# Attention and feed-forward on one core: the second feed-forward product as seven block products for each pair of batches

## Chip, core and metric

The kernel runs on one core of a Trainium2 chip. TensorE is PE in the profile, VectorE DVE, ScalarE ACT, GpSimd POOL, and SyncE, which issues all DMAs here, SP. The metric is the device time of one execution in microseconds (us).

## What is computed

Attention over 8 batches of 12 heads (448 rows of 64), and a feed-forward layer over the 3584 rows of 768 that come out of it. Everything is float32 (or float64 weights, which are decoded first). Cut to what matters here:

```python
q_n, k_n = rmsnorm(q, g_q), rmsnorm(k, g_k)
attn = softmax(q_n @ k_n.T / 8)          # 8 batches x 12 heads, 448 x 448
x = (attn @ v).reshape(3584, 768)
h = x @ w_in                             # 3584 x 2048
g = h * np.cos(h)
y = g @ w_out                            # 2048 x 768
```

## The kernel before

The program has two stages, each with its own plan. A plan (`Plan`) is a list of steps; `add` names a step's engine, its cost, when it is due, and which tiles it reads and writes. `order` plays the list through with one clock for each engine: of the steps that could start, an engine takes the one that is due first. Rings (`RING`, `RING2`) say how many buffers a kind of tile has. What comes out is a fixed order of instructions on each engine. The plan reckons the five engines as independent: a step of DVE costs the same whether POOL is at work or not. Costs are numbers written in the code (`add(DVE, 1.66, ...)`).

Products are made with float32 operands split in two float32r parts, hi and lo: ACT casts hi (`nc.scalar.copy`), POOL or DVE subtracts it from the operand for lo, and PE does three matmuls, hi by hi, hi by lo and lo by hi, into one PSUM bank.

First stage, to about 979 us: the attention, by pairs of heads, and h = x @ w_in of batches 0 to 6 fitted between (`ffn1`, lines 547 to 549, slices `fc` of 128 of the 2048 columns, 16 of them). h goes to DRAM (`h_out`, `h_store`, tile `h_d`). `weights2` brings w_out in 32 halves of a slice, decodes it (DVE, and one step of ACT), splits it (`v_split`: ACT line 261, POOL line 263) and stores both parts in DRAM (`wo_d`).

Second stage: PE begins with h of the last batch (`ffn1_block`, 16 slices of 18 matmuls of 448 columns). As each slice is through, its place in SBUF takes a slice of w_out (`v_place`, 768 KB, from `wo_d`). All 16 slices are then resident. The rows are taken in 7 groups of 512 (`CT`), whatever their batch. For each group and each two slices (a block of 128 x 1024):

- SP loads h (`gl_load`, line 569);
- `g_turns`: how many turns h is, rounded by adding a large number (DVE, line 576), made into the amount to take off (POOL, line 578);
- `g_reduce`: two instructions on DVE (lines 584 and 586) bring h to within half a turn;
- `g_cos`: absolute value and sine on ACT (lines 590, 591);
- `g_mul`: h times cosine on DVE (line 595);
- `g_split`: hi on ACT (line 604), lo on POOL (line 602);
- `ffn2` on PE (lines 618 to 620): for each slice, 6 output blocks x 3 matmuls of 512 columns, summed over 16 slices in 6 PSUM banks.

At the end of a group ACT and DVE take turns to copy the six banks (`y_out`, lines 632 and 634), and SP stores them.

Of the kernel before, what the change touches and what calls it, by code (L numbers as in the profile page):

```python
# [126 lines left out]
def tile_attention_moe(  # L127
# [115 lines left out]
    def v_fetch(fc, hf):
        cs = slice(hf * HM, hf * HM + HM)
        st = apool.tile([128, DM], I32, tag="wf", name=f"rawo{fc}_{hf}", bufs=RING["wf"])
        f = apool.tile([128, DM], F32, tag="wf", name=f"wo{fc}_{hf}", bufs=RING["wf"])
        half[(fc, hf)] = (st, f[:, :HM])
        if f64:
            nc.sync.dma_start(st, w_out[fc][:, cs].bitcast(I32))
        else:  # L250
            nc.sync.dma_start(f[:, :HM], w_out[fc][:, cs])

    def v_decode(fc, hf, step):
        st, f = half[(fc, hf)]
        if f64:
            decode(st, f, step)

    def v_split(fc, hf, lo):
        st, f = half[(fc, hf)]
        if not lo:  # L260
            nc.scalar.copy(st.bitcast(F32R)[:, :HM], f)
        else:
            nc.gpsimd.tensor_tensor(st.bitcast(F32R)[:, HM:], f, st.bitcast(F32)[:, :HM], ALU.subtract)
# [301 lines left out]
    gts = {}

    def gl_load(b, gi):
        hb = gpool.tile([128, NG, CT], F32, tag="hb", name=f"hb{b}_{gi}", bufs=4)
        nc.sync.dma_start(hb, h_d[gi * NG : gi * NG + NG, :, b * CT : b * CT + CT].rearrange("f p s -> p f s"))
        gts[(b, gi)] = {"h": hb}  # L570

    def g_turns(b, gi, step):
        d = gts[(b, gi)]
        if step == 0:
            n = d["n"] = gpool.tile([128, NG, CT], F32, tag="n", name=f"n{b}_{gi}", bufs=2)
            nc.vector.tensor_scalar(n, d["h"], 1.0 / (2.0 * math.pi), MAGIC, op0=ALU.mult, op1=ALU.add)  # L576
        else:
            nc.gpsimd.tensor_scalar(d["n"], d["n"], -MAGIC, -C1, op0=ALU.add, op1=ALU.mult)  # L578

    def g_reduce(b, gi, step):  # L580
        d = gts[(b, gi)]
        if step == 0:
# [1 line left out]
            nc.vector.tensor_tensor(r, d["h"], d["n"], ALU.add)  # L584
        else:
            nc.vector.scalar_tensor_tensor(d["r"], d.pop("n"), C2 / C1, d["r"], op0=ALU.mult, op1=ALU.add)  # L586

    def g_cos(b, gi):
        r = gts[(b, gi)]["r"]
        nc.scalar.activation(r, r, AF.Abs)  # L590
        nc.scalar.activation(r, r, AF.Sin, bias=halfpi, scale=-1.0)

    def g_mul(b, gi):
        d = gts[(b, gi)]
        nc.vector.tensor_tensor(d["r"], d["r"], d.pop("h"), ALU.mult)

    def g_split(b, gi, lo):
        d = gts[(b, gi)]
        t = gpool.tile([128, NG, CT], F32R, tag="glo" if lo else "ghi", name=f"g{lo}{b}_{gi}")
        d["lo" if lo else "hi"] = t  # L600
        if lo:
            nc.gpsimd.tensor_tensor(t, d.pop("r"), d["hi"].bitcast(F32), ALU.subtract)  # L602
        else:
            nc.scalar.copy(t, d["r"])  # L604

    ys = {}

    def ffn2(b, fc):
        d = gts[(b, fc // NG)]
        hi, lo = d["hi"][:, fc % NG, :], d["lo"][:, fc % NG, :]  # L610
        w = wts[("wo", fc)]
        for oc in range(NOC):
# [5 lines left out]
            nc.tensor.matmul(y, whi, hi, start=(fc == 0), stop=False)  # L618
# [1 line left out]
            nc.tensor.matmul(y, wlo, hi, start=False, stop=(fc == NFC - 1))  # L620
# [303 lines left out]
```

## Time and profile before

| | us |
|---|---|
| median of 3 runs (1504.03 to 1506.16) | 1504.94 |
| the profiled execution, its own time | 1502.19 |
| its span in the profile | 1500.1 |
| PE busy | 1453.1 |
| DVE busy | 1036.8 |
| ACT busy | 867.3 |
| POOL busy | 848.5 |

How to read it: a line of the page or of a group names the engine, the line of the kernel, the operation, and output <- input by the program's names; x56 is a count. Where three figures stand with strokes between, they are the shortest, the median and the longest of one instruction in ns. A window row gives its length and then, for each engine, the busy time in it and in brackets the number of instructions; the last three figures are the clock granted to PE, the share of time in which the DMA engines were busy, and what they moved in GB/s. A timeline row gives start and duration in us; in square brackets stands how long the engine was idle before it, and what ended that. Matmuls are pipelined: one of 512 columns lasts 0.39 us and the next starts 0.23 us after it. An instruction that waits inside, after it was issued, counts as busy.

### The profile page before, as it was taken

Reading aid. Unit: us, or ns where it says so; the run is one execution under the profiler, and the core shown is the slowest. Engines: PE = TensorE matmul, PEld = TensorE weight load, DVE = VectorE, ACT = ScalarE, POOL = GpSimd, SP = SyncE. Lnnn points to the kernel's source line nnn. Section 1 sums busy time; section 2 is a strip of 40 time slices with the busy share of each in tenths; the row PEclk is TensorE's granted clock in tenths of the full one; section 3 lists DMA queues with packets and bytes.
Section 4 is the critical chain, followed back from the end, with each engine's and each line's share of the span. In section 5 each row is a group of like instructions: output and inputs, shape, how many; then the busy total and the mean of one; then the engine's idle time right before and its main releaser. Section 6 shows DMA issues by size and latency. Waiting matters only on the chain.

```text
span 1500.1 us, 21753 instructions
## 1 busy us (share of the span) xinstructions
PE 1453.1 (97%) x7404; PEld 1164.9 (78%) x7404; DVE 1036.8 (69%) x1856; ACT 867.3 (58%) x1736; POOL 848.5 (57%) x678
## 2 busy tenths in 40 slices
PE   7898998999999999999999999999999999999998
PEld 3446786878788878877887888788888888888887
DVE  7878999778777777877777765452566665665660
ACT  5777777677767766766666675442343443434431
POOL 5779789766856756855655462042344444454441
PEclk8999999999999999999999999999999999999999
DMA  6576424556455555544454441177232323323221
GB/s 201 175 227 223 124 84 139 184 174 174 156 160 177 153 152 165 151 151 144 152 167 127 125 127 60 64 275 278 56 100 70 99 83 98 99 71 98 71 71 42
DMA packets 113919, 204.28 MB, mean 136 GB/s; under 512 B 19008, under 2 KB 73104, under 8 KB 113808
## 3 DMA queue, kind: packets, MB, share of 16 engines
q1 hardware_dynamic: 113808, 202.90, 43.3%
q8 instruction: 58, 0.95, 0.3%
q14 instruction: 53, 0.43, 0.1%
HBM read 149.55 MB, written 53.29 MB: 135 GB/s over the span
## 4 chain that ended last, share of the span: by engine, by line
PE 77%; DVE 6%; ACT 3%; issue 3%; POOL 2%; DMA 1%; ACTq 0%; POOLq 0%; DVEq 0%
PE y L618 10%; PE y L619 10%; PE y L620 10%; PE ph L547 9%; PE ph L548 8%; PE ph L549 8%; PE O L502 8%; PE PT L466 7%; PE S L421 6%; ACT hi L477 1%; DVE lo L485 1%; DVE S L428 1%; DVE xf L519 1%; DVE hi L487 1%; DVE wo L217 1%
## 5 line engine op out<-in xcount | busy, mean ns | idle before, releaser
L547 PE MATMUL ph<-xs,wi 128*128 128x448 f32 x768 | 298.7, 389 | 3.2 <-ACT he L559 3.2
L548 PE MATMUL ph<-xs,wi 128*128 128x448 f32 x768 | 282.1, 367 | 1.2 <-DVE xs L533 1.2
L549 PE MATMUL ph<-xs,wi 128*128 128x448 f32 x768 | 281.3, 366 | 0.0
L441 ACT ACTIVATE P<-S,sm 128x448 f32<-128x448 f32 x336 | 214.1, 641 | 100.1 <-DVE S L428 89.2
L618 PE MATMUL y<-g,wo 128*128 128x512 f32 x672 | 262.5, 391 | 0.0
L620 PE MATMUL y<-g,wo 128*128 128x512 f32 x672 | 261.5, 389 | 0.0
L619 PE MATMUL y<-g,wo 128*128 128x512 f32 x672 | 261.5, 389 | 0.0
L428 DVE TENSOR_SCALAR_CACHE_REDUCE S<-S,nr 128x448 f32<-128x448 f32 x336 | 219.4, 684 | 17.6 <-PE S L421 16.1
L602 POOL TENSOR_TENSOR g<-r,g 128x1024 fp32r<-128x1024 f32 x56 | 140.9, 2516 | 156.1 <-ACT g L604 156.0
L477 ACT CAST hi<-PT 128x448 fp32r<-128x448 f32 x336 | 164.7, 536 | 83.6 <-PE PT L466 45.5
L485 DVE TENSOR_TENSOR lo<-PT,hi 128x448 fp32r<-128x448 f32 x252 | 145.3, 617 | 77.6 <-ACT hi L477 76.7
L466 PEld LDWEIGHTS PT<-ident,P 128*128 128x128 f32 x1344 | 156.5, 141 | 33.7 <-issue 22.8
L466 PE MATMUL PT<-ident,P 128*128 128x128 f32 x1344 | 181.9, 276 | 0.1
L547 PEld LDWEIGHTS ph<-xs,wi 128*128 128x128 f32 x768 | 144.7, 188 | 34.5 <-issue 13.0
L590 ACT ACTIVATE r<-r 128x1024 f32<-128x1024 f32 x56 | 59.4, 1061 | 167.7 <-DVE r L586 167.5
L584 DVE TENSOR_TENSOR r<-hb,n 128x1024 f32<-128x1024 f32 x56 | 83.6, 1493 | 103.6 <-POOL g L602 102.3
L549 PEld LDWEIGHTS ph<-xs,wi 128*128 128x128 f32 x768 | 144.5, 188 | 12.4
L548 PEld LDWEIGHTS ph<-xs,wi 128*128 128x128 f32 x768 | 145.1, 189 | 11.4 <-DVE xs L533 2.0
L299 POOL TENSOR_TENSOR r<-r,nhalf 128x14 f32<-128x14 f32 (+1 forms) x50 | 127.4, 2550 | 40.5 <-DVE r L295 30.5
L618 PEld LDWEIGHTS y<-g,wo 128*128 128x128 f32 x672 | 126.1, 188 | 28.7 <-ACT ye L632 1.3
L578 POOL TENSOR_SCALAR n<-n 128x1024 f32<-128x1024 f32 x56 | 76.7, 1370 | 125.7 <-DVE n L576 124.6
L620 PEld LDWEIGHTS y<-g,wo 128*128 128x128 f32 x672 | 126.1, 188 | 26.3
(83 smaller groups left out, 2584.0 us busy)
## 6 DMA issues: line engine op xcount, KB each, us to landing
h_d<-he SPq DMA_DIRECT2D x128, 224.0 KB
hb<-h_d SPq DMA_DIRECT2D x56, 512.0 KB
sd<-sd SPq DMA_DIRECT2D x46, 448.0 KB
vd<-v SPq DMA_DIRECT2D x84, 160.0 KB
qd<-qT SPq DMA_DIRECT2D x48, 256.0 KB
raw<-w_in SPq DMA_DIRECT2D x16, 768.0 KB
...
```

What stands on the lines that cost most here:

```text
L428: nc.vector.tensor_scalar(d["S", t][:, :S], d["S", t][:, :S], d["nr"][:, t : t + 1], None, op0=ALU.mult, op1=ALU.min, accum_out=d["sm"][:, ...
L441: nc.scalar.activation(tl(u, f"P{t}", [128, S], F32, "P"), d.pop(("S", t))[:, :S], AF.Exp, bias=sm[:, 1, t : t + 1], scale=-1.0, accum_out ...
L466: nc.tensor.transpose(pt[:, t * 128 : t * 128 + 128], src, ident)
L477: nc.scalar.copy(hi, pt[:, hh * S : hh * S + S])
L485: nc.vector.tensor_tensor(lo, src, hi.bitcast(F32), ALU.subtract)
L547: nc.tensor.matmul(ph[:, :S], whi, x2[:, 0, :], start=(cc == 0), stop=False)
L548: nc.tensor.matmul(ph[:, :S], whi, x2[:, 1, :], start=False, stop=False)
L549: nc.tensor.matmul(ph[:, :S], wlo, x2[:, 0, :], start=False, stop=(cc == NCC - 1))
L602: nc.gpsimd.tensor_tensor(t, d.pop("r"), d["hi"].bitcast(F32), ALU.subtract)
L618: nc.tensor.matmul(y, whi, hi, start=(fc == 0), stop=False)
L619: nc.tensor.matmul(y, whi, lo, start=False, stop=False)
L620: nc.tensor.matmul(y, wlo, hi, start=False, stop=(fc == NFC - 1))
```

## The change

Batches are taken in pairs. For a pair, g is seen as a 2 x 2 matrix of blocks (which half of the 2048 columns of g; which batch), and w_out as 2 x 2 blocks (which half of its 2048 rows: X, Y; which half of its 768 columns: 1, 2). The four output blocks come from seven products of blocks instead of eight. In the code, a and b are the first half of g for the first and second batch of the pair, c and d the second half for the first and second. Products in order: a by X1; b - a by X2 + Y2; then b, now holding d - b, by X1 - X2; d, a (d less the former a), c, and a (less c) by the other three combinations and Y1, Y2. Each is 8 slices x 3 output blocks x 3 matmuls of 448 columns.

The parts of the change:

- `weights2`, first stage: for each of 8 slices, four quarter pieces are fetched and decoded as before, POOL makes four combinations (`v_mix`), and seven results are split and stored: 56 splits on ACT and on POOL, 32 mixes on POOL, 56 stores, where 32 splits and 32 stores stood.
- `v_place`: the weights of products 0 and 1 stay resident in 8 places. Those of products 2 to 6 are loaded anew for each pair into the other 8, two slices (768 KB) at a time: 16 loads at first, as before, and 72 more while the products run.
- `g_turns` is one instruction on ACT that writes an int32. DVE's line 576 and POOL's line 578 go.
- `g_reduce`, `g_cos`, `g_mul` work on blocks of 128 x 896, 64 in all. Their result stays in SBUF in float32 (tiles B, four homes of four blocks); rings: 3 buffers for h, 5 for hi, 4 for lo.
- `g_mix`: 16 blocks for each pair are combined, 12 on DVE and 4 on POOL.
- `g_split` is done for each slice of each product: 224 casts on ACT and 224 subtractions on POOL of 128 x 448.
- `e_copy` (36 on ACT), `e_add` (48 on DVE, reading PSUM) and `e_sum` (36 on DVE, both inputs in SBUF) put the outputs together.
- `h_d` is laid out by batch, and the scratch for dynamic DMA is set to 1024.

The change, cut:

```diff
-    h_d = dpool.tile([NFC, 128, B * S], F32, tag="h_d", name="h_d")
-    wo_d = dpool.tile([NFC, 128, 2, DM], F32, tag="wo_d", name="wo_d")
+    h_d = dpool.tile([B, NFC, 128, S], F32, tag="h_d", name="h_d")
+    NH = NFC // 2
+    NPR = 7
+    wo_d = dpool.tile([NH, NPR, 128, 2, HM], F32, tag="wo_d", name="wo_d")
...
+        "wx": 5, "wv": 2,
...
+    X1, X2, Y1, Y2, SS = range(5)
+    ORDER = (1, 5, 7, 3, 6, 2, 4)
...
+    def v_mix(k, to, a, c, op):
+        if to == SS and (k, SS) not in mix:
+            mix[(k, SS)] = apool.tile([128, HM], F32, tag="wx", name=f"wx{k}_{SS}", bufs=RING["wx"])
+        nc.gpsimd.tensor_tensor(mix[(k, to)], mix[(k, a)], mix[(k, c)], op)
...
+    def v_split(k, p, m, lo):
         if not lo:
-            nc.scalar.copy(st.bitcast(F32R)[:, :HM], f)
-        else:
-            nc.gpsimd.tensor_tensor(st.bitcast(F32R)[:, HM:], f, st.bitcast(F32)[:, :HM], ALU.subtract)
-
-    def v_store(fc, hf):
-        st, _ = half.pop((fc, hf))
-        cs = slice(hf * HM, hf * HM + HM)
-        nc.sync.dma_start(wo_d[fc][:, :, cs], st.bitcast(F32).rearrange("p (a n) -> p a n", a=2))
-
-    def v_place(fc):
-        w = wts[("wo", fc)] = wpool.tile([128, 2, DM], F32R, tag=f"w{fc}", name=f"wo{fc}")
-        nc.sync.dma_start(w.bitcast(F32), wo_d[fc])
+            t = vts[(k, p)] = apool.tile([128, 2, HM], F32R, tag="wv", name=f"wv{k}_{p}", bufs=RING["wv"])
+            nc.scalar.copy(t[:, 0, :], mix[(k, m)])
+        else:
+            t = vts[(k, p)]
+            nc.gpsimd.tensor_tensor(t[:, 1, :], mix[(k, m)], t.bitcast(F32)[:, 0, :], ALU.subtract)
...
+    def v_place(pr, pi, kk, slot):
+        w = wts[("wo", slot)] = wpool.tile([128, 2, 2, HM], F32R, tag=f"w{slot}", name=f"wo{pr}_{pi}_{kk}")
+        nc.sync.dma_start(w.bitcast(F32), wo_d[2 * kk : 2 * kk + 2, pi].rearrange("f p a n -> p f a n"))
...
+    def g_turns(pr, role, g):
+        n = blk[(pr, role, g, "n")] = gpool.tile([128, NG, S], I32, tag="n", name=f"n{pr}{role}{g}", bufs=RING2["n"])
+        nc.scalar.activation(n, gts[(pr, role, g)], AF.Copy, scale=1.0 / (2.0 * math.pi))
...
+            nc.vector.scalar_tensor_tensor(
+                t, blk[(pr, role, g, "n")], -C1, gts[(pr, role, g)], op0=ALU.mult, op1=ALU.add
...
+            nc.vector.scalar_tensor_tensor(t, blk.pop((pr, role, g, "n")), -C2, t, op0=ALU.mult, op1=ALU.add)
...
+    def g_mix(pr, to, a, c, g, eng):
+        t = blk[(pr, to, g)]
+        eng.tensor_tensor(t, blk[(pr, a, g)], blk[(pr, c, g)], ALU.subtract)
+
+    def g_split(pr, pi, role, k, lo):
+        t = gpool.tile([128, S], F32R, tag="glo" if lo else "ghi", name=f"g{lo}{pr}{pi}{k}", bufs=RING2["glo" if lo else "ghi"])
+        ops[(pr, pi, k, lo)] = t
+        src = blk[(pr, role, k // NG)][:, k % NG, :]
         if lo:
-            nc.gpsimd.tensor_tensor(t, d.pop("r"), d["hi"].bitcast(F32), ALU.subtract)
-        else:
-            nc.scalar.copy(t, d["r"])
-
-    ys = {}
-
-    def ffn2(b, fc):
-        d = gts[(b, fc // NG)]
-        hi, lo = d["hi"][:, fc % NG, :], d["lo"][:, fc % NG, :]
-        w = wts[("wo", fc)]
-        for oc in range(NOC):
-            if fc == 0:
-                ys[(b, oc)] = ps_y.tile([128, 512], F32, tag="y", name=f"y{b}_{oc}")
-            y = ys[(b, oc)]
+            nc.gpsimd.tensor_tensor(t, src, ops[(pr, pi, k, 0)].bitcast(F32), ALU.subtract)
+        else:
+            nc.scalar.copy(t, src)
...
+    def ffn2(pr, pi, k, slot):
+        hi, lo = ops.pop((pr, pi, k, 0)), ops.pop((pr, pi, k, 1))
+        w = wts[("wo", slot)][:, k % 2]
+        for oc in range(NO):
+            if k == 0:
+                ys[(pr, pi, oc)] = ps_y.tile([128, 512], F32, tag="y", name=f"y{pr}_{pi}_{oc}")
+            y = ys[(pr, pi, oc)][:, :S]
...
+            nc.tensor.matmul(y, whi, hi, start=(k == 0), stop=False)
             nc.tensor.matmul(y, whi, lo, start=False, stop=False)
-            nc.tensor.matmul(y, wlo, hi, start=False, stop=(fc == NFC - 1))
-
-    yes = {}
-
-    def y_out(b, oc, hf=None):
-        y = ys[(b, oc)]
-        if (b, oc) not in yes:
-            yes[(b, oc)] = gpool.tile([128, CT], F32, tag=f"ye{oc}", name=f"ye{b}_{oc}", bufs=1)
-        ye = yes[(b, oc)]
-        if hf is not None:
-            y, ye = (t[:, hf * CT // 2 : hf * CT // 2 + CT // 2] for t in (y, ye))
-        if (hf if hf is not None else oc) % 2 == 0:
-            nc.scalar.copy(ye, y)
-        else:
-            nc.vector.tensor_copy(ye, y)
-
-    def y_store(b, oc):
-        nc.sync.dma_start(out[oc * 128 : oc * 128 + 128, b * CT : (b + 1) * CT], yes.pop((b, oc)))
+            nc.tensor.matmul(y, wlo, hi, start=False, stop=(k == NH - 1))
...
+    def e_copy(pr, pi, oc, name):
+        nc.scalar.copy(e_tile(pr, name, oc), ys.pop((pr, pi, oc))[:, :S])
+
+    def e_add(pr, pi, oc, to, a, op):
+        y = ys.pop((pr, pi, oc))[:, :S]
+        if op == ALU.add:
+            nc.vector.tensor_tensor(e_tile(pr, to, oc), y, e_tile(pr, a, oc), op)
+        else:
+            nc.vector.tensor_tensor(e_tile(pr, to, oc), e_tile(pr, a, oc), y, op)
+
+    def e_sum(pr, oc, to, a, eng):
+        t = e_tile(pr, to, oc)
+        eng.tensor_tensor(t, t, e_tile(pr, a, oc), ALU.add)
...
+        todo = ((1, X1, None), (2, Y1, None), (4, Y2, None), (5, SS, (X2, Y2, ALU.add)), (7, X2, (X1, X2, ALU.subtract)),
+                (6, SS, (SS, X1, ALU.subtract)), (3, Y1, (Y1, SS, ALU.subtract)))
+        for n, (p, m, ab) in enumerate(todo):
+            e = d + n * span / 14.0
+            if ab:
+                add(POOL, 1.05, e, v_mix, k, m, *ab, r=[x[i] for i in ab[:2] if i != m], w=[x[m]])
+            t = ("wv", NPR * k + n)
+            add(ACT, 0.5, e + 3.0, v_split, k, p, m, False, r=[x[m]], w=[t])
+            add(POOL, 1.05, e + 5.0, v_split, k, p, m, True, r=[x[m]], w=[t])
+            add(SP, ISS, e + 9.0, v_store, k, p, r=[t], land=LAND)
...
+    NGR, NO = NH // NG, NOC // 2
+    ROLES = {"a": (0, 0), "b": (0, 1), "d": (1, 1), "c": (1, 0)}
+    RING2 = {"he": 2, "hb": 3, "n": 2, "ghi": 5, "glo": 4, "y": 8}
...
+    def slot(pr, pi, kk):
+        return 4 * pi + kk if pi < 2 else 8 + (20 * pr + 4 * (pi - 2) + kk) % 8
...
+    def block(pr, role, g, d):
+        i, j = ROLES[role]
+        n = next(count)
+        hb, t = ("hb", n), ("n", n)
+        B_ = ("B", home(pr, role), g)
+        r = [("hd", 2 * pr + j, NH * i + NG * g + f) for f in range(NG)]
+        add(SP, ISS, d - 30.0, gl_load, pr, role, g, r=r, w=[hb], land=LAND)
+        add(ACT, 0.95, d - 20.0, g_turns, pr, role, g, r=[hb], w=[t])
+        add(DVE, 1.15, d - 17.0, g_reduce, pr, role, g, 0, r=[hb, t], w=[B_])
+        add(DVE, 1.15, d - 16.0, g_reduce, pr, role, g, 1, r=[t], w=[B_])
+        add(ACT, 2.0, d - 14.0, g_cos, pr, role, g, w=[B_])
+        add(DVE, 1.2, d - 11.0, g_mul, pr, role, g, r=[hb], w=[B_])
...
+    def product(pr, pi, role):
+        d0 = T0 + PROD * (NPR * pr + pi)
+        for kk in range(NH // 2):
+            if pi >= 2 or pr == 0:
+                s = slot(pr, pi, kk)
+                add(SP, ISS, d0 + 2 * PART * kk - 24.0, v_place, pr, pi, kk, s, w=[("w", s)], land=8.0)
+        for k in range(NH):
+            d = d0 + PART * k
+            n = next(split_n)
+            B_, hi, lo = ("B", home(pr, role), k // NG), ("ghi", n), ("glo", n)
+            add(ACT, 0.53, d - 7.0, g_split, pr, pi, role, k, 0, r=[B_], w=[hi])
+            add(POOL, 1.25, d - 5.0, g_split, pr, pi, role, k, 1, r=[B_, hi], w=[lo])
+            s = slot(pr, pi, k // 2)
+            add(PE, PART, d, ffn2, pr, pi, k, s, r=[hi, lo, ("w", s)], w=[("y", Y(pr, pi, oc)) for oc in range(NO)])
+        return d0 + PROD
...
+    for pr in range(NPAIR):
+        D = [T0 + PROD * (NPR * pr + pi) for pi in range(NPR + 1)]
+        gs_ = range(NGR)
+        for role, pi in (("a", 0), ("b", 1), ("d", 2), ("c", 5)):
+            for g in gs_:
+                block(pr, role, g, D[pi] + BLOCK * g - (9.0 if role != "a" else 0.0))
+        copies(pr, 0, "e1", product(pr, 0, "a") + 2)
+        for g in gs_:
+            mix(pr, "a", "b", "a", g, DVE, D[1] + BLOCK * g - 10.0)
+        copies(pr, 1, "e5", product(pr, 1, "a") + 2)
+        for g in gs_:
+            mix(pr, "b", "d", "b", g, POOL, D[2] + BLOCK * g - 12.0)
+        copies(pr, 2, "e7", product(pr, 2, "b") + 2)
+        for g in gs_:
+            mix(pr, "a", "d", "a", g, DVE, D[4] + BLOCK * g - 14.0)
+        sums(pr, 3, "e3", "e5", ALU.add, product(pr, 3, "d") + 2)
+        d = product(pr, 4, "a") + 2
+        sums(pr, 4, "u", "e1", ALU.add, d)
+        more(pr, "e3", "u", d + 3, DVE, (0, 1))
+        more(pr, "e7", "u", d + 5, DVE)
+        more(pr, "e5", "e7", d + 7, DVE, (1, 1))
+        for g in gs_:
+            mix(pr, "a", "a", "c", g, DVE, D[6] + BLOCK * g - 14.0)
+        sums(pr, 5, "e1", "e1", ALU.add, product(pr, 5, "c") + 2, (0, 0))
+        sums(pr, 6, "e7", "e7", ALU.subtract, product(pr, 6, "a") + 2, (1, 0))
```

How this stands in the queues, at three places. Line numbers in the rows of after are those of the changed kernel. First POOL, in the steady part of the second stage. Before (g<-r,g is a lo split of two slices, n a turn count):

```order
L602 TENSOR_TENSOR g_0_13024<-r_0_12944,g_0_13021 128x1024
L602 TENSOR_TENSOR g_1_13073<-r_1_12993,g_1_13067 128x1024
L578 TENSOR_SCALAR n_4_13069<-n_4_13069 128x1024
L578 TENSOR_SCALAR n_5_13100<-n_5_13100 128x1024
L602 TENSOR_TENSOR g_2_13152<-r_2_13046,g_2_13147 128x1024
L578 TENSOR_SCALAR n_6_13175<-n_6_13175 128x1024
```

After, at the end of the pair's second product and the start of its third (L614 is a lo split of one slice, L607 the mix b = d - b; B0b is the block b of pair 0):

```order
L607 TENSOR_TENSOR B0b_11912<-B0d_12123,B0b_11912 128x896
L614 TENSOR_TENSOR g_12230<-B0a_11720,g_12197 128x448
L614 TENSOR_TENSOR g_12236<-B0a_11720,g_12212 128x448
L614 TENSOR_TENSOR g_12254<-B0a_11765,g_12232 128x448
L614 TENSOR_TENSOR g_12268<-B0a_11765,g_12247 128x448
L607 TENSOR_TENSOR B0b_11951<-B0d_12143,B0b_11951 128x896
L614 TENSOR_TENSOR g_12299<-B0b_11822,g_12282 128x448
L614 TENSOR_TENSOR g_12304<-B0b_11822,g_12285 128x448
```

The turn counts are gone from POOL, each split is of one slice, and a product's eight splits stand there whether its operand is new or was split before in another combination.

Second DVE, in the second stage. Before, in the order of one block after another (L584 and L586 reduce, L595 multiplies):

```order
L584 TENSOR_TENSOR r_2_13478<-hb_2_13325,n_2_13399 128x1024
L586 SCALAR_TENSOR_TENSOR r_2_13478<-n_2_13399,r_2_13478 128x1024
L576 TENSOR_SCALAR n_4_13501<-hb_4_13427 128x1024
L595 TENSOR_TENSOR r_2_13478<-r_2_13478,hb_2_13325 128x1024
L584 TENSOR_TENSOR r_3_13527<-hb_3_13356,n_3_13430 128x1024
L586 SCALAR_TENSOR_TENSOR r_3_13527<-n_3_13430,r_3_13527 128x1024
```

After, during the first products of pair 0 (L589 and L594 reduce, L603 multiplies, L607 mixes):

```order
L607 TENSOR_TENSOR B0a_11720<-B0b_11912,B0a_11720 128x896
L589 SCALAR_TENSOR_TENSOR B0d_12123<-n0d_12104,hb_6_12038 128x896
L594 SCALAR_TENSOR_TENSOR B0d_12123<-n0d_12104,B0d_12123 128x896
L589 SCALAR_TENSOR_TENSOR B0d_12143<-n0d_12126,hb_7_12079 128x896
L594 SCALAR_TENSOR_TENSOR B0d_12143<-n0d_12126,B0d_12143 128x896
L607 TENSOR_TENSOR B0a_11765<-B0b_11951,B0a_11765 128x896
L603 TENSOR_TENSOR B0d_12123<-B0d_12123,hb_6_12038 128x896
L607 TENSOR_TENSOR B0a_11597<-B0d_12008,B0a_11597 128x896
```

Every instruction there has two inputs in SBUF; the mixes stand between the blocks' own steps.

Third ACT, where PE comes to the end of `ffn1_block` (he_15 is the copy of its last slice). Before, the cosine of the fifth block (r_4) is the last one ahead of it:

```order
L590 ACTIVATE r_4_11678<-r_4_11678 128x1024
L591 ACTIVATE r_4_11678<-r_4_11678,halfpi 128x1024
L559 COPY he_10_11739<-ph_10_11684 128x448
L559 COPY he_11_11761<-ph_11_11716 128x448
L559 COPY he_12_11789<-ph_12_11742 128x448
L559 COPY he_13_11811<-ph_13_11768 128x448
L559 COPY he_14_11835<-ph_14_11792 128x448
L559 COPY he_15_11864<-ph_15_11816 128x448
```

After, the ninth (four of a, four of b, the first of d):

```order
L582 ACTIVATE n0d_12003<-hb_4_11945 128x896
L566 COPY he_13_12006<-ph_13_11953 128x448
L566 COPY he_14_12033<-ph_14_11982 128x448
L598 ACTIVATE B0d_12008<-B0d_12008 128x896
L599 ACTIVATE B0d_12008<-B0d_12008,halfpi 128x896
L582 ACTIVATE n0d_12040<-hb_5_11980 128x896
L566 COPY he_15_12055<-ph_15_12012 128x448
L616 CAST g_12073<-B0a_11720 128x448
```

More blocks, each of 896 columns where it was 1024, stand ahead of the last copy, with the first splits among them.

More of the change, by code (lines that the diff above doesn't have):

```diff
@@ L241, in tile_attention_moe, with v_fetch @@
     half = {}
[L243 to L247 removed]
+    mix = {}
+    X1, X2, Y1, Y2, SS = range(5)
+    ORDER = (1, 5, 7, 3, 6, 2, 4)
+    def v_fetch(k, m):
+        fc, cs = k + NH * (m // 2), slice(m % 2 * HM, m % 2 * HM + HM)
+        f = mix[(k, m)] = apool.tile([128, HM], F32, tag="wx", name=f"wx{k}_{m}", bufs=RING["wx"])
@@ L248, in v_fetch, with v_decode @@
         if f64:
+            st = half[(k, m)] = apool.tile([128, DM], I32, tag="wf", name=f"rawo{k}_{m}", bufs=RING["wf"])
             nc.sync.dma_start(st, w_out[fc][:, cs].bitcast(I32))
         else:
[L251 to L259, printed above, removed]
+            nc.sync.dma_start(f, w_out[fc][:, cs])
+    def v_decode(k, m, step):
+        decode(half[(k, m)], mix[(k, m)], step)
@@ L824, in tile_attention_moe @@
             multiply(b)
-    for i in range(2 * NFC):
-        weights2(*divmod(i, 2))
+    for k in range(NH):
+        weights2(k)
     with tc.manual_schedule():
@@ L837, in tile_attention_moe @@
     add = plan.add
[L838 to L839 removed]
+    BLOCK = 3.66
+    PART = BLOCK / 2.0
+    PROD = PART * NH
+    T0 = BLOCK * NFC
+    NPAIR = B // 2
     for fc in range(NFC):
@@ new lines, in slot @@
+    def slot(pr, pi, kk):
+        return 4 * pi + kk if pi < 2 else 8 + (20 * pr + 4 * (pi - 2) + kk) % 8
+    count = iter(range(1000))
+    split_n = iter(range(1000))
+    def block(pr, role, g, d):
[10 more added lines that the diff above has]
+        add(DVE, 1.2, d - 11.0, g_mul, pr, role, g, r=[hb], w=[B_])
@@ new lines, in mix @@
+    def mix(pr, to, a, c, g, eng, d):
+        e, cost = (nc.vector, 1.2) if eng == DVE else (nc.gpsimd, 2.4)
+        add(eng, cost, d, g_mix, pr, to, a, c, g, e,
+            r=[("B", home(pr, x), g) for x in (a, c) if x != to], w=[("B", home(pr, to), g)])
+    def product(pr, pi, role):
[4 more added lines that the diff above has]
+                add(SP, ISS, d0 + 2 * PART * kk - 24.0, v_place, pr, pi, kk, s, w=[("w", s)], land=8.0)
+        for k in range(NH):
+            d = d0 + PART * k
[6 more added lines that the diff above has]
+        return d0 + PROD
@@ new lines, in Y, with copies, sums @@
+    def Y(pr, pi, oc):
+        return NFC + NO * (NPR * pr + pi) + oc
+    def copies(pr, pi, name, d):
+        for oc in range(NO):
+            add(ACT, 0.53, d + oc, e_copy, pr, pi, oc, name, r=[("y", Y(pr, pi, oc))], w=[(name, oc)])
+    def sums(pr, pi, to, a, op, d, where=None):
+        for oc in range(NO):
+            add(DVE, 0.65, d + oc, e_add, pr, pi, oc, to, a, op,
+                r=[("y", Y(pr, pi, oc))] + ([(a, oc)] if a != to else []), w=[(to, oc)])
+            if where:
+                add(SP, ISS, d + oc + 1, e_store, pr, oc, to, *where, r=[(to, oc)], land=LAND)
@@ new lines, in more @@
+    def more(pr, to, a, d, eng, where=None):
+        e, cost = (nc.vector, 0.65) if eng == DVE else (nc.gpsimd, 1.25)
+        for oc in range(NO):
+            add(eng, cost, d + oc, e_sum, pr, oc, to, a, e, r=[(a, oc)], w=[(to, oc)])
+            if where:
+                add(SP, ISS, d + oc + 1, e_store, pr, oc, to, *where, r=[(to, oc)], land=LAND)
+    for pr in range(NPAIR):
[23 more added lines that the diff above has]
+        sums(pr, 6, "e7", "e7", ALU.subtract, product(pr, 6, "a") + 2, (1, 0))
```

130 lines of the change are left out of this document (54 added, 76 removed).

## Prediction

> **What bounds the kernel now.** I read the page's engine shares first, then the windows by stage, then the timeline of TensorE over the last stage, then single lines of VectorE and GpSimd there.
>
> ```profile
> PE 1453.1 (97%) x7404; PEld 1164.9 (78%) x7404; DVE 1036.8 (69%) x1856; ACT 867.3 (58%) x1736; POOL 848.5 (57%) x678
> ```
>
> ```profile
> core 0: us, PE busy (x) PEld busy (x) DVE busy (x) ACT busy (x) POOL busy (x), PEclk, DMA share, GB/s
> 222.00:849.00 627.00, 609.68 (x3431) 499.75 (x3430) 484.56 (x1055) 437.51 (x1008) 416.22 (x378) 1.00 0.51 156
> 979.00:1038.00 59.00, 57.94 (x281) 52.34 (x280) 26.45 (x21) 22.62 (x29) 19.75 (x10) 1.00 0.91 321
> 1038.00:1496.00 458.00, 458.00 (x2016) 377.26 (x2015) 260.04 (x222) 174.91 (x177) 198.18 (x102) 1.00 0.26 80
> ```
>
> PE is the bound everywhere. From 1038 on it runs the second product without one gap: 458.00 busy of 458.00. The averages of the other engines (DVE 57%, POOL 43% there) look like ample room. They aren't, as the next part shows.
>
> The timeline of PE gives the pitch of a matmul from start to start, for 448 columns (last batch of the first product) and for 512 (second product):
>
> ```profile
> 999.79 0.37 PE L549 MATMUL ph<-xs,wi 128*128 128x448 f32 x1
> ...
> 1037.61 0.37 PE L549 MATMUL ph<-xs,wi 128*128 128x448 f32 x1
> 1037.82 0.40 PE L618 MATMUL y<-g,wo 128*128 128x512 f32 x1
> ...
> 1495.42 0.39 PE L618 MATMUL y<-g,wo 128*128 128x512 f32 x1
> ...
> 1495.87 0.39 PE L620 MATMUL y<-g,wo 128*128 128x512 f32 x1
> ```
>
> L549 comes once in three matmuls, 61 times between 999.79 and 1037.61: 37.82/183 = 0.2067 us. L618 comes 671 times after its first: 457.60/2013 = 0.2273 us.
>
> **What the change takes off PE.** The old second product is 7 x 16 x 18 = 2016 matmuls of 512 columns. The new one is 28 block products x 8 x 9 = 2016 matmuls of 448. So PE's own work falls from 2016 x 0.2273 = 458.2 to 2016 x 0.2067 = 416.7 us, a gain of 41.5 us, if PE stays the bound. In units of a pair of batches: 7 products of 14.9 us, 104.2 us.
>
> **VectorE and GpSimd take turns.** These are the elementwise lines of the last stage (median in the middle of the three figures), and L533, the same split as the new one:
>
> ```profile
> L576 DVE TENSOR_SCALAR n<-hb x56: 689/694/2786, 972.5 to 1448.7; 128x1024 f32<-128x1024 f32 x56
> L584 DVE TENSOR_TENSOR r<-hb,n x56: 1212/1226/2066, 975.0 to 1460.5; 128x1024 f32<-128x1024 f32 x56
> L586 DVE SCALAR_TENSOR_TENSOR r<-n,r x56: 1210/1225/1946, 978.1 to 1461.8; 128x1024 f32<-128x1024 f32 x56
> L595 DVE TENSOR_TENSOR r<-r,hb x56: 1209/1226/2053, 993.7 to 1465.4; 128x1024 f32<-128x1024 f32 x56
> L578 POOL TENSOR_SCALAR n<-n x56: 1044/1054/1917, 973.4 to 1449.5; 128x1024 f32<-128x1024 f32 x56
> L602 POOL TENSOR_TENSOR g<-r,g x56: 2384/2490/3482, 996.1 to 1473.0; 128x1024 fp32r<-128x1024 f32 x56
> L533 POOL TENSOR_TENSOR xs<-xf,xs x44: 1131/1152/1973, 50.4 to 978.4; 128x448 fp32r<-128x448 f32 x44
> L533 DVE TENSOR_TENSOR xs<-xf,xs x4: 609/1090/1578, 974.4 to 979.3; 128x448 fp32r<-128x448 f32 x4
> L519 DVE TENSOR_TENSOR xf<-O,xf x84: 578/622/629, 141.7 to 968.2; 64x448 f32<-64x448 f32 x84
> ```
>
> The maxima lie about one partner instruction above the minima. The timelines of the two engines, DVE and then POOL, at places where they meet, show why:
>
> ```profile
> 1002.50 1.22 DVE L595 TENSOR_TENSOR r<-r,hb 128x1024 f32<-128x1024 f32 x1
> 1003.64 1.22 DVE L586 SCALAR_TENSOR_TENSOR r<-n,r 128x1024 f32<-128x1024 f32 x1
> ...
> 1010.98 1.22 DVE L584 TENSOR_TENSOR r<-hb,n 128x1024 f32<-128x1024 f32 x1
> 1012.23 1.95 DVE L586 SCALAR_TENSOR_TENSOR r<-n,r 128x1024 f32<-128x1024 f32 x1
> ...
> 1131.05 1.64 DVE L595 TENSOR_TENSOR r<-r,hb 128x1024 f32<-128x1024 f32 x1 [1.70 <-ACT r L591]
> 1132.62 2.06 DVE L584 TENSOR_TENSOR r<-hb,n 128x1024 f32<-128x1024 f32 x1
> ```
>
> ```profile
> 1011.22 1.88 POOL L578 TENSOR_SCALAR n<-n 128x1024 f32<-128x1024 f32 x1 [1.50 <-DVE n L576]
> 1013.18 3.27 POOL L602 TENSOR_TENSOR g<-r,g 128x1024 fp32r<-128x1024 f32 x1
> ...
> 1128.95 2.66 POOL L602 TENSOR_TENSOR g<-r,g 128x1024 fp32r<-128x1024 f32 x1 [2.85 <-ACT g L604]
> 1131.70 1.91 POOL L578 TENSOR_SCALAR n<-n 128x1024 f32<-128x1024 f32 x1
> ```
>
> Follow them one after another: L584 to 1012.20; then L578, issued at 1011.22, ends at 1013.10, 0.90 us after L584; then L586 to 1014.18; then L602 to 1016.45, 2.27 us after L586. The same at 1131: L602 ends 1131.61, L595 1132.69, L578 1133.61, L584 1134.68. Wherever both want to work on SBUF operands, one stands still until the other is done. L519, whose first input is in PSUM, never exceeds 629 ns in 84 times, so it is exempt. The Trainium skill, page "SBUF — State Buffer", section "Who interferes with whom", says this of a DVE instruction with two SBUF inputs and a GpSimd instruction that reads SBUF: whoever starts first holds a shared port for its whole instruction. The trace agrees in kind, but a waiting instruction overlaps about 0.1 us of it.
>
> So the two engines are one resource in this stage. Its load before, per block of two slices: DVE 0.694 + 1.226 + 1.225 + 1.226 = 4.371, POOL 1.054 + 2.490 = 3.544, together 7.915; times 56 blocks 443 us, of PE's 458. The old kernel just fits.
>
> **The same sum for the change.** New instructions of 128x896 are priced by 896/1024 of the rows.
> - Removed: L576 and L578 (turn count), 56 x 1.748 = 97.9 us; ScalarE makes the turn count now.
> - Reduction and multiply on DVE: 64 blocks x 3 x 1.073 (1.226 x 0.875). No row has one int32 input among two; I take L586's price. The mixes on DVE (3 x 4 groups x 4 pairs) add 48 x 1.073. Together 240 x 1.073 = 257.5 us.
> - Output sums with both inputs in SBUF: 36 on DVE at L533's 0.609 = 21.9 us. The 48 other output sums read a product from PSUM, as L519 does, and don't count here.
> - Splits on POOL: every block product splits its operand anew, 28 x 8 = 224 x 1.152 = 258.0 us, where 56 x 2.490 = 139.4 stood.
> - Mixes on POOL: 16 x 2.490 x 0.875 = 34.9 us.
>
> Sum 572.3 us, where 443 stood and PE now needs only 416.7. From below: independent DVE instructions follow each other at 1.14 (1002.50 to 1003.64) for 1.226, and the blocked L602 took 2.27 for 2.490, so 0.93 x 279.4 + 0.91 x 292.9 = 527 us. I take 572, because neither queue is always ready: in-order waits give back what the overlap saves. By the page's rule, held for the whole instruction, the sum would be 572 too; by the rows alone 527.
>
> **What is done ahead.** In the new order of ScalarE nine of the first pair's 16 blocks have their cosine ahead of the last h copy, so by 1038 the shared port may have done 9 x 3 x 1.073 + 2 mixes + 5 splits = 37 us of it. DMA is at a 0.91 share in that window and brings the same weight bytes and more h; if only the five blocks of the old order are through it is 20 us. I take 30. A new wait stands there: on POOL the mix b = d - b comes between the fourth and the fifth split of the first product, and waits for d's block, so for an h load of that full window, a reduction, a cosine and a multiply. Queued behind it is the fifth split, and behind that PE. The four splits ahead cover 4 x 1.86 = 7.4 us of PE's time; what d comes later than that would be lost to PE, but the port goes on with blocks meanwhile, so I charge nothing beyond the 30 instead of 37.
>
> **The other engines** fit under 143 us per pair (572/4). ScalarE, by these rows:
>
> ```profile
> L288 ACT ACTIVATE sd<-sd 128x896 f32<-128x896 f32 x46 | 44.0, 957 | 3.1 <-DMA sd<-sd 3.1
> ```
>
> ```profile
> L590 ACT ACTIVATE r<-r x56: 1050/1062/1067, 990.1 to 1463.1; 128x1024 f32<-128x1024 f32 x56
> L591 ACT ACTIVATE r<-r,halfpi x56: 1151/1153/1158, 992.5 to 1464.2; 128x1024 f32<-128x1024 f32 x56
> L531 ACT CAST xs<-xf x48: 554/568/597, 49.8 to 977.7; 128x448 fp32r<-128x448 f32 x48
> ```
>
> 16 x (0.957 + 0.93 + 1.01) + 65 x 0.568 = 83 us. DMA per pair: 20 weight loads of 0.786 MB, 16 h loads of 0.459, 12 stores of 0.229, 25.8 MB; at the 321 GB/s of the window 979 to 1038 that is 80 us. SP issues them in order; a weight load waits there for PE to leave its slot, with h loads queued behind it, but a slot comes free 26 us (two products less two slices) ahead of its next use.
>
> **The first stage.** Weight splits go from 32 to 56 on POOL, with 32 mixes added:
>
> ```profile
> L263 POOL TENSOR_TENSOR rawo<-wo,rawo x32: 992/1010/1038, 258.5 to 885.0; 128x384 fp32r<-128x384 f32 x32
> ```
>
> 56 more instructions of 1.010 = 57 us on POOL (66% busy in 222 to 849), 24 more casts on ScalarE, 24 more stores on SP. PE misses only 17.3 us in that window, so most of it hides; if that cover went, up to 57. I take 4, between -2 (another order) and 20.
>
> **The sum.** 1037.8 + (572.3 - 30) = 1580.1 for the last split; then eight matmuls (1.7) and the end as now (1500.1 - 1495.87 = 4.2): 1586. With 4 for the first stage 1590 of span, 2.1 around it (1502.19 against 1500.1), and 2.75 by which the median of 1504.94 lies over the profiled run: 1595 us, some 6% slower. Lower end: 527 - 37, first stage -2: 1536. Upper end: only 20 done ahead, and in half of the 64 blocks nothing uses the port while ScalarE does abs and sine (64 x 1.94 = 124, half 62): 1666.
>
> **Rivals.**
> - Faster: the splits run beside DVE as L519 does, PE stays the bound. 1504.94 - 41.5 + 4 = 1467. The 57% and 43% speak for it, every meeting in the trace against it. It decides if DVE and POOL really overlap by more than 572 - 30 - 417 = 125 us. 0.08.
> - An overlap of about 90 us (1595 - 1505) would end within 3 us of now: 0.02.
> - Slower still: the three queues, in a fixed order that reckons DVE and POOL as independent, wait in a ring: ScalarE on a reduction, POOL on ScalarE's cast, DVE on ScalarE's cosine. All 124 us lost: up to 1719. Before, L595's waits for L591 were 1.65 us each, but POOL used them. 0.09.
> - Slower by DMA: streamed weights in 3 KB pieces at the 156 GB/s of the first stage take 165 us per pair, +22 x 4: 1683. The 321 of the nearer window speaks against it. 0.03.
>
> The forecast itself has 0.78. A measurement here tells 0.2% apart. Faster 0.08, same 0.02, slower 0.90. The range 1536 to 1666 leaves out the faster cases and most of the two slower ones.
>
> **What would show it.** After 1038, PE busy near 417 of about 545 us, its waits ending on POOL's splits; means of the DVE reductions well over 1.073 and of POOL's splits well over 1.152, with minima at these values; their clean times summing to nearly the whole stage; a pair about 143 us long, where 104 means the first rival. Full-length DVE and POOL instructions lying side by side unstretched would prove the whole argument wrong; waits on DMA from wo or hb, the last rival.

## The result and the profile after

The changed kernel takes 1553.28 us (median of 4 runs, 1550.64 to 1554.98) against 1504.49 us before (median of 4): 1.0324 times as long, 95% interval 1.0303 to 1.0346. The forecast was 1595 with a range of 1536 to 1666, so the direction and the place are right and the size is too large by 42 us. The profiled execution took 1550.64 us, its span is 1548.9.

The page's line of engine shares, and the windows of the profile after, first over most of the first stage, then over the end of the first product, three stretches of the second product, and all of the second product:

```profile
PE 1441.8 (93%) x7404; PEld 1180.7 (76%) x7404; DVE 1224.9 (79%) x1935; ACT 993.9 (64%) x2022; POOL 1109.0 (72%) x862
```

```profile
222.00:849.00 627.00, 606.71 (x3411) 499.59 (x3409) 495.02 (x1059) 446.32 (x1029) 475.42 (x435) 0.99 0.55 173
```

```profile
979.00:1038.00 59.00, 59.00 (x288) 53.57 (x287) 33.81 (x31) 38.10 (x52) 8.33 (x6) 1.00 0.91 318
1038.00:1143.00 105.00, 94.57 (x426) 81.31 (x425) 96.08 (x60) 63.41 (x95) 88.88 (x49) 0.95 0.51 176
1143.00:1270.00 127.00, 110.26 (x488) 96.02 (x486) 119.92 (x80) 75.87 (x113) 105.54 (x59) 0.93 0.58 203
1270.00:1400.00 130.00, 111.95 (x501) 96.69 (x500) 121.45 (x80) 74.38 (x112) 107.62 (x60) 0.95 0.57 193
1038.00:1546.00 508.00, 448.31 (x2021) 391.27 (x2019) 437.70 (x296) 278.29 (x421) 413.75 (x236) 0.95 0.54 185
```

The first stage has 59 us more on POOL (475.42 against 416.22) and costs almost nothing. The second product lasts 506 us (1038.8 to 1545.2) where it was 458. By the starts of their first matmuls, the four pairs take 128, 130, 131 and 117 us, where PE's own work is 104. In the stretch of 127 us from 1143 on DVE is busy 94% and POOL 83%: together 225 us in 127, since an instruction that is held up by the other engine counts as busy too.

The lines of the stage show that. First POOL's splits and DVE's steps, then two kinds of output sum on DVE, which differ only in where their first input lies (L651 reads y from PSUM, L657 has both inputs in SBUF). The three figures are shortest, median and longest in ns:

```profile
L614 POOL TENSOR_TENSOR g<-B0a,g x32: 1135/1990/2012, 992.6 to 1160.5; 128x448 fp32r<-128x448 f32 x32
L614 POOL TENSOR_TENSOR g<-B1a,g x32: 1149/1996/2024, 1164.1 to 1290.3; 128x448 fp32r<-128x448 f32 x32
...
```

```profile
L589 DVE SCALAR_TENSOR_TENSOR B0a<-n0a,hb x4: 1091/1092/1093, 984.7 to 1005.2; 128x896 f32<-128x896 int32 x4
...
L589 DVE SCALAR_TENSOR_TENSOR B0c<-n0c,hb x4: 1720/2032/3011, 1066.5 to 1089.5; 128x896 f32<-128x896 int32 x4
...
```

```profile
L657 DVE TENSOR_TENSOR es<-es x24: 611/1570/1580, 1137.3 to 1521.6; 128x448 f32<-128x448 f32 x24
...
```

```profile
L651 DVE TENSOR_TENSOR es<-y,e x24: 605/610/625, 1117.8 to 1516.0; 128x448 f32<-128x448 f32 x24
L651 DVE TENSOR_TENSOR e<-y,e x12: 607/617/625, 1152.5 to 1530.6; 128x448 f32<-128x448 f32 x12
```

A split whose shortest time is 1.14 us has a median of 1.99. A reduction takes 1.09 us before 1038, where POOL has little to do, and 2.03 (the median of the block shown) after. The sums that read PSUM stay within 605 to 625 ns in the midst of it; the same sum with both inputs in SBUF has a median of 1570.

The two timelines side by side, DVE first, at one place of the second pair:

```profile
1192.16 2.04 DVE L607 TENSOR_TENSOR B1a<-B1d,B1a 128x896 f32<-128x896 f32 x1
1194.12 3.00 DVE L589 SCALAR_TENSOR_TENSOR B1c<-n1c,hb 128x896 f32<-128x896 int32 x1
1197.15 1.90 DVE L594 SCALAR_TENSOR_TENSOR B1c<-n1c,B1c 128x896 f32<-128x896 int32 x1
1198.97 2.04 DVE L607 TENSOR_TENSOR B1a<-B1d,B1a 128x896 f32<-128x896 f32 x1
```

```profile
1193.21 2.96 POOL L607 TENSOR_TENSOR B1b<-B1d,B1b 128x896 f32<-128x896 f32 x1
1196.13 3.93 POOL L614 TENSOR_TENSOR g<-B1a,g 128x448 fp32r<-128x448 f32 x2
```

Read the ends: DVE's mix 1194.20, POOL's mix 1196.17, DVE's reduction 1197.12, POOL's first split about 1198.1, DVE's second reduction 1199.05, POOL's second split 1200.06, DVE's next mix 1201.01. POOL's mix takes two microseconds of its own, each of the others about one, and they alternate without a gap.

PE's waits in the second product, by the chain of releasers:

```profile
PE y L628 <- POOL g L614: 47.5, 31, 3.7
PE y L627 <- ACT g L616: 11.4, 6, 3.4
```

PE waits 59 us in all, and 47.5 of these for the lo splits. No wait for weights or h stands there.

### The profile page after: what moved, and what is told of

Same layout as the page of the kernel before. It is cut to its first block, busy times and chain, and to the rows that moved or that the text cites. A ratio compares the mean times of both kernels' runs of the same rounds, so it can differ in the third digit from the quotient of the medians.

```text
span 1548.9 us, 23023 instructions
## 1 busy us (share of the span) xinstructions
PE 1441.8 (93%) x7404; PEld 1180.7 (76%) x7404; DVE 1224.9 (79%) x1935; ACT 993.9 (64%) x2022; POOL 1109.0 (72%) x862
## 5 line engine op out<-in xcount | busy, mean ns | idle before, releaser
L628 PE MATMUL y<-g,wo 128*128 128x448 f32 x672 | 262.9, 391 | 47.5 <-POOL g L614 47.5
L627 PE MATMUL y<-g,wo 128*128 128x448 f32 x672 | 254.5, 379 | 11.4 <-ACT g L616 11.4
L629 PE MATMUL y<-g,wo 128*128 128x448 f32 x672 | 254.3, 378 | 0.0
L628 PEld LDWEIGHTS y<-g,wo 128*128 128x128 f32 x672 | 132.3, 197 | 79.7 <-POOL g L614 69.2
L627 PEld LDWEIGHTS y<-g,wo 128*128 128x128 f32 x672 | 132.1, 197 | 25.4 <-ACT g L616 13.6
L629 PEld LDWEIGHTS y<-g,wo 128*128 128x128 f32 x672 | 132.4, 197 | 10.4
L509 PE MATMUL O<-hi,vs 128*128 128x448 f32 x336 | 111.9, 383 | 8.4 <-DVE hi L494 5.2
L509 PE MATMUL O<-lo,vs 128*128 128x448 f32 x252 | 99.6, 404 | 17.0 <-DVE lo L492 16.5
L371 POOL TENSOR_TENSOR kl<-kd,khi 128x448 fp32r<-128x448 f32 x46 | 55.7, 1210 | 67.1 <-ACT khi L367 67.0
```

The source lines that it names most:

```text
L509: nc.tensor.matmul(O, st, d.pop((what, kb, hh)), start=(kc + n == 0), stop=(kc + n == 4))
L627: nc.tensor.matmul(y, whi, hi, start=(k == 0), stop=False)
L629: nc.tensor.matmul(y, wlo, hi, start=False, stop=(k == NH - 1))
```

## The experiments

All start from the changed kernel, but for the last two. A time without an interval is one run.

**Splits that only write.** The lo split becomes writes of zeros of about the same length.

```diff
-            nc.gpsimd.tensor_tensor(t, src, ops[(pr, pi, k, 0)].bitcast(F32), ALU.subtract)
+            nc.gpsimd.memset(t.bitcast(F32), 0.0)
+            nc.gpsimd.memset(t.bitcast(F32), 0.0)
+            nc.gpsimd.memset(t.bitcast(F32)[:, :S // 2], 0.0)
```

> Each lo split on GpSimd is replaced by writes of zeros of about the same time in all (two of 448 columns and one of 224), which read nothing from SBUF; the lo parts of the activations are left out of the result. If VectorE and GpSimd take turns at SBUF operands (my theory), VectorE's reductions fall back to about 1.09 us each and TensorE runs nearly without waits: about 1467 to 1480 us. If GpSimd's own time or its place in the chain of a split is what binds, or the streamed weights, or ScalarE's added work, the time stays near 1553.

1457.29 us. The window of the second pair, and two lines:

```profile
1143.00:1247.00 104.00, 104.00 (x515) 96.37 (x514) 82.87 (x84) 78.78 (x116) 79.95 (x173) 1.00 0.75 255
```

```profile
L589 DVE SCALAR_TENSOR_TENSOR B0c<-n0c,hb x4: 1080/1088/1092, 1062.8 to 1079.4; 128x896 f32<-128x896 int32 x4
...
```

```profile
L614 POOL MEMSET g<- x224: 468/473/490, 974.4 to 1444.4; 128x448 f32 x112
```

POOL works for 80 of 104 us, more than the 73 that its splits and mixes would need alone, ScalarE does all its work, DMA moves 255 GB/s with all the weights in it, and PE doesn't miss a microsecond. What the changed kernel lacks isn't POOL's time, nor ScalarE's, nor DMA's. What is left is that the splits read SBUF, or that they wait for ScalarE's cast; the next run takes these apart.

**The same, with the chain kept.** In that run POOL no longer waited for ScalarE's cast. Here it does:

```diff
+            nc.gpsimd.tensor_tensor(t[:, :32], src[:, :32], ops[(pr, pi, k, 0)].bitcast(F32)[:, :32], ALU.subtract)
+            nc.gpsimd.memset(t.bitcast(F32)[:, 32:], 0.0)
+            nc.gpsimd.memset(t.bitcast(F32)[:, 32:], 0.0)
```

> As the run with writes only, but GpSimd makes the real lo for the first 32 of 448 columns and then writes zeros to the other 416 twice, so that it waits for ScalarE's cast as in the changed kernel and takes as long as there; lo is left out for the 416. Taking turns: the short real part holds the shared access some 0.2 us instead of 1.0, so 1460 to 1475 us. If the first run with writes got its gain because GpSimd no longer waited for ScalarE's cast (the chain cast, split, TensorE): near 1553.

1471.07 us. PE's only waits in the second product:

```profile
PE y L630 <- POOL g L616: 7.1, 9, 1.4
```

So the chain from cast to split to PE and the short read together cost 14 us, and not the 96 us (1553.28 - 1457.29) that lie between the two kernels.

**No streaming.** `if pr == 0 and pi < 4` in place of `if pi >= 2 or pr == 0` ahead of `v_place`.

> The weights of the seven products are loaded only once into the 16 places and never again, so products use weights that are not theirs; 72 loads of 768 KB are gone, everything else is unchanged. Taking turns (my theory): no change, 1550 to 1556 us. If the streamed weights, or the queue of SP behind them, take the time: faster by up to 85 us, to about 1470.

1557.21 us: no gain. The splits are stretched as before:

```profile
L614 POOL TENSOR_TENSOR g<-B1a,g x32: 1136/1994/2014, 1167.8 to 1293.8; 128x448 fp32r<-128x448 f32 x32
```

The rival of the weights' transfers falls.

**Without DVE's mixes.**

```diff
-        eng.tensor_tensor(t, blk[(pr, a, g)], blk[(pr, c, g)], ALU.subtract)
+        if eng is nc.gpsimd:
+            eng.tensor_tensor(t, blk[(pr, a, g)], blk[(pr, c, g)], ALU.subtract)
```

> The 48 mixes on VectorE are left out, so products take operands that were not combined; the order of everything else is unchanged. Taking turns: 48 instructions of 1.0 us net are missing from a resource that is used for 97% of the stage, so about 45 us less: 1505 to 1515 us, with GpSimd's splits still stretched to a median near 1.9 us. If GpSimd alone were the bound, no change (1553); if the dependence of each product on the mixes before it were (latency, not load), TensorE would run free: below 1490.

1512.59 us, 41 less for 48 instructions: 0.85 us each. Taking work from DVE makes PE wait less for POOL: 31.5 us in the second product where it was 47.5.

**One reduction for two.** `-C1 - C2` in the first, and the second goes from the plan.

> The two reductions of a block on VectorE become one, with 2 pi as one float32 constant in place of its two parts; 64 instructions of 128x896 are gone, nine of them from before the second product. Taking turns: 55 x 0.98 = 54 us less, about 1499 us, with the splits still stretched. If latency in the chain of a block were the limit, more than that; if GpSimd alone, nothing.

1509.43 us, 44 less where 54 were expected; 0.8 us for each of the 55. From the first matmul of the second product to the last split, one of the two engines at least is at work on SBUF operands in 433 of 457 us here (95%), in 441 of 464 in the run before (95%), and in 483 of 500 in the changed kernel (97%).

**The plan's costs.** DVE's block steps and mixes 1.95, POOL's splits 2.0, its mixes 2.95, PE's slice 2.25.

> The same work; only the plan's numbers are changed to the durations that the trace of the changed kernel shows (VectorE 1.95 for each block step and mix, GpSimd 2.0 for a split and 2.95 for a mix, 2.25 for TensorE's slice), so the fixed orders come out differently. If the load of the two engines that take turns is what binds (97% used), an order can win at most the 3% that are idle and the start: 1540 to 1560 us. If the order, made as though they were independent, is the cause: below 1525.

1547.94 us, 1.0295 times the kernel before (1.0277 to 1.0312), where the changed kernel is at 1.0324 (1.0303 to 1.0346). The intervals overlap: an order made with the durations as they are gains 5 us if anything.

**Splits on DVE.**

```diff
-            nc.gpsimd.tensor_tensor(t, src, ops[(pr, pi, k, 0)].bitcast(F32), ALU.subtract)
+            nc.vector.tensor_tensor(t, src, ops[(pr, pi, k, 0)].bitcast(F32), ALU.subtract)
-            add(POOL, 1.25, d - 5.0, g_split, pr, pi, role, k, 1, r=[B_, hi], w=[lo])
+            add(DVE, 0.62, d - 5.0, g_split, pr, pi, role, k, 1, r=[B_, hi], w=[lo])
```

> The 224 lo splits go from GpSimd to VectorE, planned there at 0.62 us; nothing is left out. Taking turns: a split occupies the shared access for about 0.55 us in place of 1.0, so after 1038 us VectorE has 240 x 1.0 + 36 x 0.55 + 224 x 0.55 + 48 x 0.62 = 413 us, GpSimd's mixes 16 x 2.0 = 32, less 32 done ahead: 413 us against TensorE's 417. About 1475 to 1495 us, faster than both kernels. If VectorE and GpSimd worked side by side, VectorE would now have 445 us by itself where it had 320, and the time would rise or stay: 1553 or more.

1502.62 us (ratio to the kernel before 0.9997, 0.9985 to 1.0010): 51 us less than the changed kernel with more work on the busier engine, which two engines at work side by side could not give. But it isn't the 1475 to 1495 that was expected. A window within the second pair and one line of POOL:

```profile
1143.00:1247.00 104.00, 93.34 (x439) 82.91 (x438) 95.23 (x117) 64.53 (x97) 10.79 (x4) 0.98 0.61 199
```

```profile
L607 POOL TENSOR_TENSOR B0b<-B0d,B0b x4: 2129/2680/14195, 1040.5 to 1073.0; 128x896 f32<-128x896 f32 x4
```

In the second product DVE is busy 415 us, as reckoned, and PE needs 417. I set the larger of the two as the time, but the product lasts 457: DVE is at 92% in this window, PE at 90%. They wait for each other: PE 33.9 us in all for DVE's splits, and DVE's splits 17.9 us for PE to leave a buffer. That this is the whole of the difference isn't shown.

**Everything on DVE.** As in the last run, and POOL's 16 mixes of b as well.

> The lo splits and the 16 mixes of GpSimd all on VectorE, two reductions as in the changed kernel; GpSimd does nothing in the second product. VectorE alone by full durations: 256 x 1.09 + 36 x 0.62 + 224 x 0.62 + 48 x 0.61 = 470 us, some 36 ahead of time: 434 against TensorE's 417, so about 1495 to 1515 us. If the mixes left on GpSimd (one of 14 us in the run with splits on VectorE) are what kept that run from 1480: below 1490.

1502.77 us (0.9990, 0.9976 to 1.0005), inside the expected range. Taking the mixes off POOL, that of 14 us with them, gains nothing on balance: DVE has 17 us more to do for it. How much of either the other cancels isn't shown.

**Splits on DVE and one reduction.** Both edits from above together.

> Both edits, lo splits on VectorE and one reduction: VectorE by full durations has 176 x 1.09 + 36 x 0.62 + 224 x 0.62 + 48 x 0.61 = 382 us, about 26 of it ahead of time, and GpSimd's mixes take 16 x 2 more: under TensorE's 417. Taking turns: TensorE becomes the bound again, 1460 to 1475 us, 2 to 3% faster than the kernel before. If something else than these two engines holds the second product back: 1490 or more.

1479.49 us, 0.9842 times the kernel before (0.9817 to 0.9866). This is the fastest version that does all of the work (its only difference in the numbers is one constant for 2 pi). The second and the third pair:

```profile
1143.00:1247.00 104.00, 104.00 (x510) 95.39 (x509) 92.56 (x121) 74.61 (x112) 15.84 (x4) 1.00 0.74 243
1247.00:1351.00 104.00, 96.10 (x463) 86.02 (x463) 88.99 (x113) 70.12 (x105) 9.50 (x4) 1.00 0.65 219
```

PE is full in the second pair and loses 8 us in the window of the third. The time is 4 us above the 1475 expected at most. The kernel before wasn't run with one reduction or with its splits on DVE, so how much of this gain comes from the seven products isn't shown.

**The kernel before, with one more instruction for each block.** First with two inputs in SBUF:

```diff
+            nc.vector.scalar_tensor_tensor(d["r"], d["n"], 0.0, d["r"], op0=ALU.mult, op1=ALU.add)
             nc.vector.scalar_tensor_tensor(d["r"], d.pop("n"), C2 / C1, d["r"], op0=ALU.mult, op1=ALU.add)
```

> The kernel before, with one more instruction per block on VectorE (zero times n added to r, 128x1024, two inputs in SBUF), which changes no value. VectorE and GpSimd together then have 443 + 56 x 1.23 = 512 us by full durations, 475 by the net times (527/572), less some 20 to 30 ahead of time, against TensorE's 458. Taking turns: TensorE begins to wait; 1505 to 1535 us. If the two engines worked side by side, VectorE would have 314 of 458 us and GpSimd 198: no change, 1500 to 1507.

1571.82 us, well over the 1535 expected at most. Then with one input:

```diff
+            nc.vector.tensor_reduce(scr, d["r"].rearrange("p f s -> p (f s)"), axis=AX.X, op=ALU.add)
             nc.vector.scalar_tensor_tensor(d["r"], d.pop("n"), C2 / C1, d["r"], op0=ALU.mult, op1=ALU.add)
```

> The kernel before, with a sum over r's 1024 columns into an unused column on VectorE, at the place of the extra instruction of the last run and about as long, but with a single input in SBUF. If the extra 1.23 us counted there as load of the access that VectorE and GpSimd share: this one doesn't, GpSimd can work beside it, and the time is near the kernel before, 1502 to 1525 us. If it counted as length of the chain from one block's step to the next on VectorE and ScalarE: near 1570 again.

1568.57 us, the same. The added instruction does leave the shared access alone: nine of the 56 overlap a split of POOL, and none is stretched.

```profile
L587 DVE TENSOR_REDUCE scr<-r x56: 1204/1220/1221, 982.5 to 1531.7; 128x1 f32<-128x1024 f32 x56
```

So here my theory was wrong: in the kernel before, it's not the shared access that is full. One of the two engines at least is at work on SBUF operands in 386 of the 438 us from the first matmul of the second product to the last split, 88%. The timelines of this last run, DVE, ACT and POOL, over one block:

```profile
1272.26 1.23 DVE L585 TENSOR_TENSOR r<-hb,n 128x1024 f32<-128x1024 f32 x1 [3.58 <-POOL g L604]
1273.52 1.22 DVE L587 TENSOR_REDUCE scr<-r 128x1 f32<-128x1024 f32 x1
1274.78 1.22 DVE L588 SCALAR_TENSOR_TENSOR r<-n,r 128x1024 f32<-128x1024 f32 x1
1276.04 0.69 DVE L577 TENSOR_SCALAR n<-hb 128x1024 f32<-128x1024 f32 x1
1278.38 1.23 DVE L597 TENSOR_TENSOR r<-r,hb 128x1024 f32<-128x1024 f32 x1 [1.65 <-ACT r L593]
1281.89 1.22 DVE L585 TENSOR_TENSOR r<-hb,n 128x1024 f32<-128x1024 f32 x1 [2.29 <-POOL g L604]
```

```profile
1276.09 1.06 ACT L592 ACTIVATE r<-r 128x1024 f32<-128x1024 f32 x1 [6.34 <-DVE r L588]
1277.19 1.15 ACT L593 ACTIVATE r<-r,halfpi 128x1024 f32<-128x1024 f32 x1
1278.25 1.03 ACT L606 CAST g<-r 128x1024 fp32r<-128x1024 f32 x1
```

```profile
1279.37 2.49 POOL L604 TENSOR_TENSOR g<-r,g 128x1024 fp32r<-128x1024 f32 x1 [1.42 <-ACT g L606]
```

DVE's first step on a block waits for POOL's split of an earlier one, whose buffer r it takes over (there are two). That split waits for a cast, which on ScalarE stands behind the cosine of the newer block, and that cosine waits for DVE's reduction. It is one ring through three engines: 9.63 us from 1272.26 to 1281.89. In the kernel before, the same ring shows on DVE as

```profile
1117.77 1.23 DVE L584 TENSOR_TENSOR r<-hb,n 128x1024 f32<-128x1024 f32 x1 [2.29 <-POOL g L602]
...
1126.14 1.23 DVE L584 TENSOR_TENSOR r<-hb,n 128x1024 f32<-128x1024 f32 x1 [2.29 <-POOL g L602]
```

8.37 us, where PE needs 36 x 0.2273 = 8.18. Nobody is stretched in the rounds shown. One instruction more between the first step and the last reduction makes such a round 1.26 us longer, whatever it reads, and 56 x 1.26 = 71 us is near what both runs show (64 to 68). Rounds aren't all alike: from 1050 on they average 8.21 us in the kernel before (6.0 to 10.6), at PE's pace, and 9.56 in the last run. PE meets the delay in one place, early in each group but the first, where DVE's copies of the output banks stand in its queue behind the steps that are late:

```profile
PE y L620 <- DVE ye L636: 51.5, 6, 9.5
```

A run that shortens the ring and leaves the work as it is wasn't made.

## Why the prediction was right, and where not

**TensorE's own work** falls to what was reckoned. With the splits out of the way it takes 1457 us, where the rival for that case said 1467; the 41.5 us are there to be had, and a little more. The second product takes 411 us there, against 417 reckoned.

**VectorE and GpSimd take turns: right.** This is the mechanism that was forecast, and no luck was needed for it. The alternation is in the timelines. Writes in place of reads give back 96 us (82 with the chain kept), and work taken from VectorE shortens PE's waits for GpSimd. The sums from PSUM are exempt. The page "SBUF — State Buffer" of the Trainium skill, section "Who interferes with whom", holds in both its halves here: two inputs in SBUF against a GpSimd instruction that reads (2.03 us for 1.09), and no contention with one that only writes (1.088).

**The price was the term that was mis-sized.** I took the full duration of each instruction (572 us) over the net one (527), "because neither queue is always ready". The timelines show that one of them nearly always is: adding up the timeline rows of both, at least one of the two has such an instruction at work in 482 of the 499 us from 1039 to 1538, 97%. A mix takes 2.0 us of its own and a split or a reduction 0.95 to 1.0, as in the alternation above, so the net times were the right ones. 527 less some 33 done ahead (at net prices too) is 494 us; the last split of the changed kernel starts at 1537.9, and with its 1.15 us ends 500 after the second product began (1038.8). I had 542, and a pair at 143 us where they take 117 to 131. The lower end of the range, 1536, was the sum by net times.

**What was done ahead:** 36 us by full durations (29 steps and mixes at 1.073, four splits at 1.152), not 30. Eight blocks were through at 1038 and the ninth in its multiply, as the order of ScalarE has it, though DMA was at a 0.91 share. The wait that I named there, POOL's first mix ahead of the fifth split, cost nothing: the mix ends at 1041.9, the split at 1043.8, and PE's first wait of any length begins at 1061.95.

**The first stage:** 1 us, not 4. The first matmul of the second product starts at 1038.81, where it was 1037.82. In the nine edits of the changed kernel, whose first stage is as there, that start lies anywhere from 1037.1 to 1042.2, so 1 and 4 can't be told apart.

**The rivals.** Faster: needs an overlap of 125 us that doesn't exist; the run with writes only shows that case. Fixed orders that lock: 17 of 499 us is all that they cost, and the order with true costs agrees. Transfers: the run without streaming gains nothing.

**One sign failed.** I named PE busy near 417 us; it is busy 448 in the second product. The clock granted to it is at a half in 51 of these us, which is some 26 us of its work. Since the two engines are at work in all but 17 us of the stage, the time can owe no more than that to it.

**"The old kernel just fits" rests on the wrong reason.** The sum of 443 us by full durations was rightly added, but the two engines are at work in 88% of the stage, so it isn't what the kernel was close to. The two runs with one more instruction point to the ring of one block. The forecast for the changed kernel didn't use it.
